# A start list written anew: two attention tiles turned by VectorE and DMA instead of TensorE, and scalings and low words on GpSimd

## The chip, the cores and the metric

The kernel runs on one core of a Trainium2 chip. Five engines work side by side, each through its own list of instructions in order: TensorE (PE; its weight loads are shown apart as PEld), VectorE (DVE), ScalarE (ACT), GpSimd (POOL) and SyncE (SP), which here only issues DMAs. ScalarE and GpSimd issue some DMAs too. The metric is the device time of one execution in microseconds (us). Before the change the median of 3 runs is 477.7 us (477.04 to 478.3).

## The reference

Attention within chunks of 64 positions, then a feed-forward layer on all 4608 tokens:

```
q, k, v: (8, 8, 576, 64)  ->  9 chunks of 64 positions per batch and head
scores = q_c @ k_c^T / 8 ;  attn = exp(scores - max) / (sum + 1e-9) ;  out = attn @ v_c
x = out as (4608, 512)
h = x @ w_in (512 x 1024) ;  e = exp(h - max) ;  sm = e / (sum e + 1e-9)
solu = h * sm ;  ln = (solu - mean) / sqrt(var + 1e-6) * g_ln
result = ln @ w_out (1024 x 512)
```

The weights arrive as 8-byte floats, 4 MB each. q, k and v are float32.

## The kernel before

The 4608 tokens are 36 tiles of 128 (two chunks of 64 each). Each tile goes through: turning q and k so that the head dimension lies on partitions; scores (64 small TensorE products); softmax; turning the probabilities; products with V; a split of x into a high and a low part; the input product (`ffn_in`, 24 TensorE products of 512 columns: high times low weights, high times high, low times high); the SoLU and its normalisation; turning z; a split of z; and the output product (`ffn_out`, 24 products, in three thirds).

There are two ways to turn. TensorE multiplies by a unit matrix into PSUM, and ScalarE or VectorE copies the outcome out. Or VectorE transposes blocks of 32 x 32 and DMAs put the blocks in place. Probabilities of the tiles below `PE_TURNED` go the first way (`attn_transpose`, word T: four TensorE transposes and four ScalarE copies per tile), the others the second (`attn_turn`, word U: one VectorE transpose per tile, and after an odd tile eight DMAs for the pair, four issued by SyncE and four by GpSimd).

From tile 5 on a loop issues the work, the same for every pair of tiles. Everything before it is issued in the order of a list, `START`: each word is a step with its tile or unit number, and a word that stands several times continues the same step. Every engine keeps the order of the list for its own instructions, its DMA issues among them. The words that matter here:

- `P:x` load weight unit x (units 0 to 3 are w_in, 4 to 7 w_out; 1 MB each); `c:x` clamp and scale it (VectorE or GpSimd, then ScalarE), `b:x` its low bits, `C:x` join, `t:x` its high word (ScalarE), `d:x` its low word;
- `n:i` load q and k of tile i as they lie in memory (`nat`, two halves used in turn), `N:i:0` and `N:i:1` turn q and k by TensorE and evict; `v:i` load V (four buffers);
- `S:i` scores, `A:i` softmax up to exp, `B:i` sum, reciprocal and scaling by it, `V:i` product with V, then the high and the low part of x;
- `M:i` input product (unit by unit for tile 0), `X:i`, `Y:i`, `R:i` SoLU, centring and variance, `z:i:h` turn half h of z by TensorE (tiles 0 and 1), `Z:i` turn z by VectorE and DMA (after tile 3: 16 DMAs), `F` the next third of an output product, `o:i` scale and store;
- `Q:2`, `q:8` the loads of q and k of batch 2 by head (`q_st`, `k_st`: 32 DMAs of 72 KB), which the tiles from 9 on read; `K:9` turns tile 9 from them;
- `w:n` n products of the unit matrix that nobody reads; `g`, `G` load and turn g_ln.

`MOVED` names the engine of some steps, where a default would be another: for evictions (N, z, V) ScalarE, for `Y` centring ScalarE, for c, b and d VectorE. `F` stands six times, so the loop starts when tiles 0 and 1 are through their output product. `ffn_in` of every tile but 1 uses one PSUM buffer (`ph`), which the multiplication in `Y` of the tile before sets free. The store of `o:i` is issued on ScalarE's own queue, in order with its other work, in the start; in the loop SyncE issues it.

In the profile almost every instruction stands under line 54, the helper through which they are recorded, so the tiles' names tell the steps apart: `nat`, `q_st`, `k_st`, `w_raw` (P), `w_a`, `w_b` (c, b, C), `wi_l`, `wo_l` (d), `sx`, `e`, `s_e` (S, A, B), `tp` (TensorE transposes and, in the loop, odd tiles' scores), `a_b` and `attn_t` (probabilities turned), `ph` (input product), `z`, `z_b`, `z_t`, `z_h`, `z_l` (z and its parts), `po` (output product).

Of the kernel before, what the change touches and what calls it, by code (L numbers as in the profile page):

```python
# [15 lines left out]


START = """
n:0 w:3 N:0:0 N:0:0 w:1 N:0:1 N:0:1 g w:1 S:0 A:0 G P:0 P:0 n:1 A:0 c:0 c:0 w:3 N:1:0 N:1:0 w:1
N:1:1 b:0 N:1:1 G P:1 w:1 S:1 B:0 v:0 C:0 A:1 t:0 T:0 T:0 c:1 c:1 w:4 V:0 V:0 P:2 b:1 c:2 n:2  # L20
d:0 P:3 A:1 n:3 w:6 N:2:0 w:1 N:2:1 C:1 V:0 B:1 t:1 c:2 T:1 N:2:0 b:2 N:2:1 T:1 d:1 S:2 n:4
M:0 M:0 C:2 t:2 c:3 c:3 v:1 A:2 A:2 b:3 d:2 C:3 N:3:0 N:3:1 N:3:1 M:0 N:3:0 S:3 N:4:0 B:2 N:4:1
t:3 N:4:0 A:3 P:5 d:3 c:5 N:4:1 A:3 T:2 T:2 S:4 V:1 M:0 P:4 n:5 B:3 T:3 V:1 V:1 M:1 X:0 X:0 T:3
A:4 A:4 b:4 v:2 N:5:1 c:4 n:6 P:7 c:5 N:5:0 c:4 Y:0 Y:0 n:7 N:5:1 V:2 b:5 v:3 B:4 N:5:0 V:2 b:7
C:4 z:0:1 P:6 v:5 N:6:0 X:1 v:4 C:5 N:6:0 S:5 Q:2 q:8 t:4 V:2 d:4 N:6:1 N:6:1 X:1 t:5 A:5 Y:1
M:2 z:0:1 z:0:1 X:2 A:5 R:0 z:0:0 z:0:0 q:8 N:7:1 q:8 c:6 S:6 Y:1 V:3 X:2 T:4 T:4 z:0:0 d:5 F
V:3 Y:2 Y:2 N:7:0 A:6 c:6 c:7 V:3 b:6 B:5 C:6 n:8 N:7:0 M:3 R:1 c:7 q:8 N:7:1 C:7 T:5 z:1:0 t:6
T:5 S:7 t:7 d:6 X:3 X:3 d:7 V:4 V:4 Y:3 Y:3 R:2 z:1:1 A:6 F F A:7 V:4 z:1:0 z:1:0 v:6 Z:2 A:7
M:4 F B:7 Z:3 o:0 V:5 z:1:1 z:1:1 B:6 F F v:7 X:4 N:8:0 X:4 U:6 U:7 V:5 Y:4 V:5 K:9 Y:4 N:8:0
R:4 R:3 N:8:1 N:8:1 o:1  # L30
"""


MOVED = """
N:0:0=dve N:8:0=dve N:8:1=dve Y:0=pool Y:1=pool Y:3=pool b:7=pool c:0=pool c:1=pool c:2=pool
c:3=pool c:4=pool c:5=pool c:6=pool c:7=pool
"""


# [23 lines left out]
def chunk_attention_then_solu_ffn(  # L63
# [18 lines left out]
    G = S // 32  # L82
# [5 lines left out]


    MS = nc.gpsimd  # L90
    PE_TURNED = 6
    PH2 = (1,)
    ORD = 5

# [12 lines left out]
    def po():  # L107
# [120 lines left out]
    def unit_low(x):  # L228
        kind, m = UNITS[x]
        a, top = scaled.pop(x), tops.pop(x)  # L230
        if kind == "in":
            dve.tensor_tensor(
                out=paired(wi_l[:, m, :]),
                in0=a.rearrange("p h (a b x) -> p (h a) x b", b=P, x=2),
                in1=top.bitcast(F32), op=ALU.subtract,
            )
            return
        for y in range(2):
            dve.scalar_tensor_tensor(
                out=wo_l[:, 2 * m + y, :], in0=a[:, y],  # L240
                scalar=g_sb[:, 2 * m + y:2 * m + y + 1], in1=top[:, y].bitcast(F32),
                op0=ALU.mult, op1=ALU.subtract,
            )
# [473 lines left out]
    def warm(n):  # L717
# [32 lines left out]
    for i in range(first, NT):  # L750
# [99 lines left out]
```

## Time and profile before

| | |
|---|---|
| median of 3 runs | 477.7 us |
| the profiled execution's own time | 477.95 us |
| its span from first to last instruction | 476.2 us |
| TensorE busy | 465.6 us (98%) |
| VectorE busy | 374.3 us (79%) |
| ScalarE busy | 256.5 us (54%) |
| GpSimd busy | 147.7 us (31%) |
| granted TensorE clock | 1.0 |
| DMA | 72.57 MB, 152 GB/s on average |

Of a group of instructions the page gives the engine, the operation, output and input by tile name, shapes and count, then the busy time and the mean of one in ns, then the engine's idle time ahead of them and what ended it. A row of the timeline has start, length, engine (SPq, POOL and ACTq for DMA issues), the same names and a count, and in brackets the idle time before it and who ended it. The row "DMA to landing" gives the time from an issue to the arrival of its data.

### The profile page before, as it was taken

What the parts mean: (1) busy time and instruction counts of PE and PEld (TensorE: products, weight loads), DVE (VectorE), ACT (ScalarE), POOL (GpSimd) and SP (SyncE); (2) the same over time, 40 slices, a digit from 0 to 9 for tenths busy, and PEclk for the clock granted to TensorE, in tenths of its full rate; (3) what the DMA queues carried; (4) which work ended last, traced back from release to release, by engine and by line L of the source; (5) the groups of instructions that cost most, each with busy time, mean ns of one, the idle gap of its engine ahead of it and who ended that gap; (6) DMA issues with size and microseconds to landing.
All of it is one profiled execution on the core that took longest, in us unless ns stands there. A gap on an engine that the chain in (4) does not pass through costs nothing.

```text
span 476.2 us, 11114 instructions
## 1 busy us (share of the span) xinstructions
PE 465.6 (98%) x4212; PEld 382.6 (80%) x4212; DVE 374.3 (79%) x520; ACT 256.5 (54%) x423; POOL 147.7 (31%) x298
## 2 busy tenths in 40 slices
PE   7899998999999999999999999999999999999997
PEld 5677786888888888888888888888888888888876
DVE  3999997798869887878787878797979797954441
ACT  2879982646444645454545455454555554545552
POOL 2212725150505050505050505032414141423330
PEclk9999999999999999999999999999999999999999
DMA  8999979758886878696358596949743435343221
GB/s 221 308 288 220 202 134 199 166 154 154 200 144 162 158 175 166 164 168 154 88 138 159 136 185 144 182 110 188 156 115 97 126 90 135 85 116 104 74 60 73
DMA packets 192924, 72.57 MB, mean 152 GB/s; under 512 B 177188, under 2 KB 177960, under 8 KB 191976
## 3 DMA queue, kind: packets, MB, share of 16 engines
q1 hardware_dynamic: 185768, 58.23, 55.4%
q0 software_dynamic: 6528, 12.86, 10.4%
q8 instruction: 33, 0.54, 0.5%
q10 hardware_dynamic: 576, 0.79, 0.5%
q14 instruction: 19, 0.16, 0.1%
HBM read 36.70 MB, written 9.44 MB: 97 GB/s over the span
## 4 chain that ended last, share of the span: by engine, by line
PE 85%; DMA 6%; SPq 3%; DVE 3%; ACT 1%; issue 1%; ACTq 0%
PE po L54 38%; PE ph L54 38%; PE tp L54 5%; PE sx L54 4%; SPq L54 3%; DMA nat<-in_k_dram 2%; DMA nat<-in_q_dram 2%; DMA z_t<-z_b 1%; DMA k_st<-in_k_dram 1%; DVE h_nmax L54 0%; DVE w_a L54 0%; DVE wo_l L54 0%; ACT attn_t L54 0%; ACT z L54 0%; ACT z_h L54 0%
## 5 line engine op out<-in xcount | busy, mean ns | idle before, releaser
L54 PE MATMUL ph<-wi_l,x_h 128*128 128x512 f32 x288 | 112.9, 392 | 1.9 <-DVE z L54 1.8
L54 PE MATMUL po<-wo_l,z_h 128*128 128x512 f32 (+1 forms) x288 | 113.3, 393 | 0.1
L54 ACT ACTIVATE z<-ph,h_nmax 128x1024 f32<-128x1024 f32 x36 | 40.2, 1117 | 134.6 <-DVE h_nmax L54 134.6
L54 PE MATMUL ph<-wi_h,x_h 128*128 128x512 f32 x288 | 112.1, 389 | 0.0
L54 PE MATMUL po<-wo_h,z_l 128*128 128x512 f32 (+1 forms) x288 | 111.9, 389 | 0.0
L54 PE MATMUL po<-wo_h,z_h 128*128 128x512 f32 (+1 forms) x288 | 111.4, 387 | 0.0
L54 POOL DMA_DIRECT2D z_t<-z_b x144 | 71.7, 505 | 28.7 <-DVE z_b L54 24.5
L54 PE MATMUL ph<-wi_h,x_l 128*128 128x512 f32 x288 | 78.1, 390 | 0.0
L54 POOL TENSOR_TENSOR u<-ssq,eps 128x1 f32<-128x1 f32 x36 | 7.1, 198 | 212.1 <-ACT sq L54 211.9
L54 DVE TENSOR_REDUCE h_nmax<-ph 128x1 f32<-128x1024 f32 x36 | 44.0, 1221 | 30.2 <-PE ph L54 30.2
L54 PEld LDWEIGHTS ph<-wi_l,x_h 128*128 128x128 f32 x288 | 54.1, 188 | 13.8 <-ACT x_h L54 2.2
L54 PEld LDWEIGHTS po<-wo_h,z_l 128*128 128x128 f32 x288 | 54.1, 188 | 12.1 <-DVE z_l L54 1.0
L54 PEld LDWEIGHTS po<-wo_l,z_h 128*128 128x128 f32 x288 | 54.1, 188 | 11.9 <-ACT z_h L54 0.5
L54 PEld LDWEIGHTS ph<-wi_h,x_l 128*128 128x128 f32 x288 | 53.9, 188 | 11.6 <-DVE x_l L54 0.4
L54 PEld LDWEIGHTS ph<-wi_h,x_h 128*128 128x128 f32 x288 | 54.1, 188 | 11.0
L54 PEld LDWEIGHTS po<-wo_h,z_h 128*128 128x128 f32 x288 | 54.1, 188 | 10.5
L54 DVE TENSOR_TENSOR z_l<-z_t,z_h 128x1024 fp32r<-128x1024 f32 (+1 forms) x37 | 42.0, 1136 | 25.3 <-ACT z_h L54 23.9
L54 DVE SCALAR_TENSOR_TENSOR z<-ph,z 128x1024 f32<-128x1024 f32 x36 | 43.9, 1219 | 13.3 <-ACT z L54 13.2
L54 ACT ACTIVATE z<-z,z_sum 128x1024 f32<-128x1024 f32 x33 | 38.1, 1154 | 23.0 <-DVE z L54 22.4
L54 DVE STREAM_TRANSPOSE z_b<-z 128x1024 f32<-128x1024 f32 x34 | 41.2, 1211 | 3.8 <-ACT z L54 3.1
L54 ACT CAST z_h<-z_t 128x1024 fp32r<-128x1024 f32 (+1 forms) x37 | 35.9, 970 | 8.6 <-PE po L54 6.5
L54 ACT ACTIVATE o_sb<-po,r 128x512 f32<-128x512 f32 (+1 forms) x36 | 24.2, 673 | 24.9 <-POOL r L54 18.6
(76 smaller groups left out, 598.6 us busy)
## 6 DMA issues: line engine op xcount, KB each, us to landing
out_dram<-o_sb SPq DMA_DIRECT2D x33, 256.0 KB, 2.5
v_sb<-in_v_dram SPq DMA_DIRECT2D x32, 256.0 KB, 4.4
z_t<-z_b POOLq DMA_DIRECT2D x128, 64.0 KB, 2.8
z_t<-z_b SPq DMA_DIRECT2D x128, 64.0 KB, 2.9
q_st<-in_q_dram SPq DMA_DIRECT2D x96, 72.0 KB, 3.1
k_st<-in_k_dram SPq DMA_DIRECT2D x96, 72.0 KB, 3.1
w_raw<-in_moe_w_out_dram SPq DMA_DIRECT2D x4, 1024.0 KB, 7.4
attn_t<-a_b POOLq DMA_DIRECT2D x60, 64.0 KB, 3.8
```

The source lines that it names most:

```text
L54: ins = make(*args, **kwargs)
```

## The change

Four things. `PE_TURNED` goes from 6 to 4, so the probabilities of tiles 4 and 5 are turned by `attn_turn`; U:4 and U:5 enter the list for T:4 and T:5. The scaling in `softmax_b` and the low word of a w_in unit in `unit_low` can be put on GpSimd by `MOVED`, which does that for B:0 to B:6, d:1 and d:3. Other entries of `MOVED` change: the clamps of units 1 and 3 go from GpSimd to VectorE, the bits of unit 4 go to GpSimd and those of unit 7 to VectorE, the centring of tile 1 to ScalarE and of tiles 3 and 4 to VectorE, some evictions change sides (N:0:1, N:1:1, N:3:0, z:1:0 and z:1:1 to VectorE, N:0:0 and N:8:1 to ScalarE). And the whole list is in another order: weight unit 1 is loaded first, unit 0 after unit 2; the loads of tile 8 (n:8) stand behind the loads of batch 2 by head; v:7 stands ahead of them; 21 unit products (w) instead of 22.

```
+START = P:1 n:0 c:1 c:1 n:1 w:6 N:0:0 b:1 w:1 N:0:1 N:0:0 P:2 C:1 t:1 w:1 N:1:0 N:1:0 N:0:1 S:0 N:1:1
+N:1:1 n:2 A:0 A:0 P:0 P:0 d:1 w:5 S:1 N:2:0 c:2 c:2 N:2:0 b:2 w:1 N:2:1 N:2:1 B:0 A:1 w:1 T:0
+C:2 b:0 c:0 A:1 T:0 S:2 c:0 g G A:2 A:2 B:1 G v:0 C:0 n:3 w:4 V:0 V:0 t:2 B:2 t:0 P:3 N:3:0
+N:3:0 n:4 w:1 N:3:1 N:3:1 v:1 T:1 T:1 V:0 T:2 S:3 d:0 b:3 M:0 T:2 c:3 A:3 N:4:0 n:5 c:3 C:3
+N:4:0 N:4:1 N:4:1 M:0 A:3 V:1 S:4 v:2 d:2 M:0 t:3 V:1 N:5:0 N:5:1 P:5 d:3 M:0 A:4 A:4 N:5:0
+N:5:1 B:3 P:4 V:1 S:5 B:4 c:5 X:0 c:4 V:2 P:6 X:0 T:3 A:5 A:5 b:5 Y:0 Y:0 c:5 M:1 z:0:0 z:0:1
+U:4 V:2 V:2 C:5 v:3 T:3 M:2 n:6 b:4 N:6:1 R:0 n:7 N:6:0 c:4 B:5 z:0:1 V:3 X:1 P:7 z:0:1 z:0:0
+z:0:0 C:4 t:5 X:1 N:7:0 t:4 v:4 Y:1 c:6 N:7:1 Y:1 v:7 N:6:1 N:6:0 d:4 N:7:0 v:5 c:7 U:5 S:6
+z:1:1 X:2 X:2 d:5 c:6 F V:3 Y:2 R:1 b:6 N:7:1 b:7 V:3 Q:2 q:8 q:8 M:3 Y:2 v:6 C:6 A:6 c:7 t:6
+q:8 q:8 C:7 d:6 t:7 S:7 X:3 V:4 d:7 z:1:0 V:4 X:3 V:4 A:6 n:8 Y:3 Y:3 F F z:1:0 z:1:0 Z:2 B:6
+A:7 o:0 z:1:1 z:1:1 R:3 Z:3 A:7 M:4 X:4 X:4 V:5 B:7 Y:4 U:6 F F U:7 Y:4 V:5 V:5 F R:2 o:1 N:8:0
+K:9 N:8:0 N:8:1 N:8:1 R:4

 MOVED = """
-N:0:0=dve N:8:0=dve N:8:1=dve Y:0=pool Y:1=pool Y:3=pool b:7=pool c:0=pool c:1=pool c:2=pool
-c:3=pool c:4=pool c:5=pool c:6=pool c:7=pool
+B:0=pool B:1=pool B:2=pool B:3=pool B:4=pool B:5=pool B:6=pool N:0:1=dve N:1:1=dve N:3:0=dve
+N:8:0=dve Y:0=pool Y:3=dve Y:4=dve b:4=pool c:0=pool c:2=pool c:4=pool c:5=pool c:6=pool
+c:7=pool d:1=pool d:3=pool z:1:0=dve z:1:1=dve

-    PE_TURNED = 6
+    PE_TURNED = 4

 (unit_low)
-            dve.tensor_tensor(
+            (pool if f"d:{x}" in moved else dve).tensor_tensor(
                 out=paired(wi_l[:, m, :]),

 (softmax_b)
-        dve.tensor_tensor(
+        (pool if f"B:{i}" in moved else dve).tensor_tensor(
             out=a, in0=e, in1=rinv.unsqueeze(2).to_broadcast([P, H, CH]), op=ALU.mult,
         )
```

The list before:

```
n:0 w:3 N:0:0 N:0:0 w:1 N:0:1 N:0:1 g w:1 S:0 A:0 G P:0 P:0 n:1 A:0 c:0 c:0 w:3 N:1:0 N:1:0 w:1
N:1:1 b:0 N:1:1 G P:1 w:1 S:1 B:0 v:0 C:0 A:1 t:0 T:0 T:0 c:1 c:1 w:4 V:0 V:0 P:2 b:1 c:2 n:2
d:0 P:3 A:1 n:3 w:6 N:2:0 w:1 N:2:1 C:1 V:0 B:1 t:1 c:2 T:1 N:2:0 b:2 N:2:1 T:1 d:1 S:2 n:4
M:0 M:0 C:2 t:2 c:3 c:3 v:1 A:2 A:2 b:3 d:2 C:3 N:3:0 N:3:1 N:3:1 M:0 N:3:0 S:3 N:4:0 B:2 N:4:1
t:3 N:4:0 A:3 P:5 d:3 c:5 N:4:1 A:3 T:2 T:2 S:4 V:1 M:0 P:4 n:5 B:3 T:3 V:1 V:1 M:1 X:0 X:0 T:3
A:4 A:4 b:4 v:2 N:5:1 c:4 n:6 P:7 c:5 N:5:0 c:4 Y:0 Y:0 n:7 N:5:1 V:2 b:5 v:3 B:4 N:5:0 V:2 b:7
C:4 z:0:1 P:6 v:5 N:6:0 X:1 v:4 C:5 N:6:0 S:5 Q:2 q:8 t:4 V:2 d:4 N:6:1 N:6:1 X:1 t:5 A:5 Y:1
M:2 z:0:1 z:0:1 X:2 A:5 R:0 z:0:0 z:0:0 q:8 N:7:1 q:8 c:6 S:6 Y:1 V:3 X:2 T:4 T:4 z:0:0 d:5 F
V:3 Y:2 Y:2 N:7:0 A:6 c:6 c:7 V:3 b:6 B:5 C:6 n:8 N:7:0 M:3 R:1 c:7 q:8 N:7:1 C:7 T:5 z:1:0 t:6
T:5 S:7 t:7 d:6 X:3 X:3 d:7 V:4 V:4 Y:3 Y:3 R:2 z:1:1 A:6 F F A:7 V:4 z:1:0 z:1:0 v:6 Z:2 A:7
M:4 F B:7 Z:3 o:0 V:5 z:1:1 z:1:1 B:6 F F v:7 X:4 N:8:0 X:4 U:6 U:7 V:5 Y:4 V:5 K:9 Y:4 N:8:0
R:4 R:3 N:8:1 N:8:1 o:1
```

More of the change, by code (lines that the diff above doesn't have):

```diff
@@ L18 @@
 START = """
[L19 to L30, printed above, removed]
+P:1 n:0 c:1 c:1 n:1 w:6 N:0:0 b:1 w:1 N:0:1 N:0:0 P:2 C:1 t:1 w:1 N:1:0 N:1:0 N:0:1 S:0 N:1:1
```

## The prediction

> **What bounds the kernel now.** I read the busy table first, then the chain of waits in order of time, then the start alone on each engine.
>
> ```profile
> PE 465.6 (98%) x4212; PEld 382.6 (80%) x4212; DVE 374.3 (79%) x520; ACT 256.5 (54%) x423; POOL 147.7 (31%) x298
> ```
>
> ```profile
> 82.15 5.68 PE ph L54 x24
> 87.83 0.72 PE sx L54 x34
> ...
> 90.27 5.70 PE po L54 x24
> ...
> 444.72 5.45 PE ph L54 x24
> ```
>
> From 82.15 us, the first product of tile 5 (first step of the loop, which the change leaves alone), the chain is TensorE piece upon piece. So the end moves with two instants: when tile 5's first product may start, and whether the products of tiles 6 and 7 with V (88.28) and the next output product (90.27) follow without a hole. Everything edited lies ahead of that.
>
> SyncE's queue is the other thing that arrives at 88 us. Its issues in the timeline (start, length):
>
> ```profile
> 50.29 0.80 SPq L54 DMA_DIRECT2D v_sb<-in_v_dram  x1
> 51.20 12.81 SPq L54 DMA_DIRECT2D q_st<-in_q_dram  x16
> 64.11 4.22 SPq L54 DMA_DIRECT2D k_st<-in_k_dram  x8
> 68.44 0.45 SPq L54 DMA_DIRECT2D nat<-in_q_dram  x1
> 69.41 0.67 SPq L54 DMA_DIRECT2D nat<-in_k_dram  x1
> 70.13 6.02 SPq L54 DMA_DIRECT2D k_st<-in_k_dram  x8
> 76.95 6.82 SPq L54 DMA_DIRECT2D z_t<-z_b  x8
> 83.87 0.53 SPq L54 DMA_DIRECT2D v_sb<-in_v_dram  x1
> 84.58 2.47 SPq L54 DMA_DIRECT2D attn_t<-a_b  x4
> ```
>
> ```profile
> DMA to landing us min/median/max: 2.0/2.5/2.9
> ```
>
> The second fence is for those four attn_t issues: the last starts near 86.5 and lands near 88.5, just when TensorE's products of tiles 6 and 7 want it. So SyncE's queue, not only TensorE, is on time to within a few tenths. Ahead of 55 us the transfers themselves are full, behind it the issue sets the pace (columns: stretch, length, busy PE, PEld, DVE, ACT, POOL, clock, DMA share, GB/s):
>
> ```profile
> 40.00:41.00 1.00, 0.45 (x4) 0.48 (x5) 0.93 (x4) 0.81 (x1) 1.00 (x1) 1.00 0.20 43
> 50.00:55.00 5.00, 5.00 (x90) 4.14 (x88) 4.38 (x8) 4.19 (x11) 2.57 (x4) 1.00 1.07 289
> 60.00:65.00 5.00, 4.82 (x87) 4.04 (x87) 5.00 (x7) 4.71 (x10) 0.64 (x1) 1.00 0.73 117
> ```
>
> **The change part by part.** *Tiles 4 and 5.* Two groups of four TensorE transposes go, and eight ScalarE copies (two groups of 1.5 us):
>
> ```profile
> 52.06 0.66 PE L54 MATMUL tp<-ident,s_e 128*128 128x128 f32 x4
> 52.48 0.48 PE L54 MATMUL po<-wo_l,z_h 128*128 128x512 f32 x1
> 52.76 1.51 ACT L54 COPY attn_t<-tp 64x256 f32<-64x256 f32 x4
> 79.41 1.29 DVE L54 STREAM_TRANSPOSE a_b<-e 128x512 f32<-128x512 f32 x2
> ```
>
> From start to next start a group costs TensorE 0.42 us, so both 0.84 us. In their place come two VectorE block transposes (the last row, 1.29 us) and eight DMAs, four on SyncE (2.47 us by the row above), four on GpSimd.
>
> *Work moved from VectorE to GpSimd and back.* Rows:
>
> ```profile
> L54 DVE TENSOR_TENSOR s_e<-e,s_rinv 128x512 f32<-128x512 f32 x6 | 4.2, 692 | 0.2
> L54 DVE TENSOR_TENSOR wi_l<-w_a,wi_h 128x1024 fp32r<-128x1024 f32 x4 | 4.9, 1216 | 0.0
> L54 POOL TENSOR_SCALAR w_a<-w_raw 128x1024 f32<-128x1024 f32 x8 | 10.3, 1289 | 31.0 <-DMA w_raw<-in_moe_w_in_dram 18.4 <-DMA w_raw<-in_moe_w_out_dram 10.3 <-DVE z L54 2.3
> L54 POOL TENSOR_SCALAR w_b<-w_raw 128x1024 uint32<-128x1024 uint32 x1 | 3.7, 3729 | 6.6 <-DVE s_nmax L54 6.6
> L54 DVE TENSOR_SCALAR w_b<-w_raw 128x1024 uint32<-128x1024 uint32 x7 | 5.9, 841 | 0.3 <-DMA w_raw<-in_moe_w_in_dram 0.3
> ```
>
> VectorE gives up seven scalings and two low words: at most 7 x 0.69 + 2 x 1.22 = 7.3 us. It takes two clamps (at its own w_b row 0.84 each), two z evictions and one more N eviction (0.69), two centrings (0.84 to 1.22) and U:4, U:5 (1.3): 7 us. So VectorE's total is unchanged; what changes is the order. GpSimd has no two-input row of this size; by its one-input rows a scaling of 512 lies between 0.64 (half of 1289) and 1.86 (half of 3729), a low word of 1024 between 1.3 and 3.7. I take 1.2 and 2.3, nearer the clamp because both are float: 13 us on an engine that is busy under a third. The scaling stands between exp and the transpose, so each costs its attention chain 0.5 us more than on VectorE; it is hidden as long as TensorE has other list work, and it has.
>
> [...]
>
> ```profile
> 36.82 1.48 DVE L54 TENSOR_SCALAR w_b<-w_raw 128x1024 uint32<-128x1024 uint32 x1
> 39.36 0.68 DVE L54 TENSOR_SCALAR w_b<-w_raw 128x1024 uint32<-128x1024 uint32 x1
> ```
>
> ```profile
> 36.65 1.10 POOL L54 TENSOR_SCALAR w_a<-w_raw 128x1024 f32<-128x1024 f32 x1 [1.47 <-DMA w_raw<-in_moe_w_out_dram]
> ```
>
> *The new order on TensorE.* Unit 0 is now loaded after units 1 and 2 and tiles 0 to 2, as the last of 4.5 MB. The page's slices of 11.9 us moved
>
> ```profile
> GB/s 221 308 288 220 202 134 199 166 154 154 200 144 162 158 175 166 164 168 154 88 138 159 136 185 144 182 110 188 156 115 97 126 90 135 85 116 104 74 60 73
> ```
>
> so 221 x 11.9 = 2.6 MB in the first, and the other 1.9 MB take 6.2 us at 308: its bytes are in at some 18.1 us, near 18.5 with the landing. VectorE's list then holds b:0, A:2 (two operations), the sums and reciprocals of B:1 and B:2, C:0, an eviction, V:0 and d:0: by 0.69 for what is 512 wide, 1.22 for 1024, 0.2 for a reciprocal, 0.7 + 1.4 + 1.8 + 1.2 + 0.7 + 0.7 + 1.2 = 7.7 us. So the first product starts near 26 us, against 23.36:
>
> ```profile
> 23.36 0.50 PE L54 MATMUL ph<-wi_l,x_h 128*128 128x512 f32 x1
> 34.21 0.48 PE L54 MATMUL ph<-wi_l,x_h 128*128 128x512 f32 x1
> 40.55 1.06 PE L54 MATMUL tp<-ident,nat 128*128 128x128 f32 x8 [0.62 <-DMA nat<-in_k_dram]
> 41.55 0.69 PE L54 MATMUL sx<-attn_t,v_sb 64*64 64x64 f32 x32
> 42.17 0.66 PE L54 MATMUL tp<-ident,z 128*128 128x128 f32 x4
> 82.15 0.47 PE L54 MATMUL ph<-wi_l,x_h 128*128 128x512 f32 x1 [1.84 <-DVE z L54]
> ```
>
> Tile 1's product (34.21 before) comes near 37, 2.8 us later; but by then N:5, V:2 and S:5 are done, which stood behind it (1.00 and 0.62 us from start to start, S:5 taken as V:2), T:4 and T:5 are gone (0.84), and the waits of 1.84 and 0.62 us need not recur. TensorE itself could thus start tile 5's product at 82.15 + 2.8 - 2.2 - 0.8 - 2.5 = 79.4; if the first product is as early as before but for a us, 77.6.
>
> *The new order on SyncE.* This decides. Into the list ahead of the 32 head loads (q_st, k_st) come v:7 and U:5's four issues; n:8 goes from between them to behind all of them. Up to 55 us bytes count: v:7 is 0.25 MB and U:5 0.5 MB, at the 289 GB/s above 0.9 + 1.7 us. A dry moment like 40:41 (share 0.20) loses 0.8 us; before, SyncE had to wait for a tile half still unread, and the new list asks for the halves later against their reading. I count 1.9 us given back; none and four such moments (3.3 us) are the ends. So the head loads start 0.7 us later, -0.7 to +2.6. They keep 0.53 us each (4.22 over 8). With n:8 not between them they end 1.8 us earlier (68.3 to 70.13), which n:8 spends again before the z_t issues; these shift by +0.7, and the split of tile 2 that wants them begins only at 88.31 now, 4 us behind the last of them. The attn_t issues lose v:7 ahead of them (84.58 - 83.77 = 0.8) and with less backlog some of the 1.5 us by which 70.13's eight exceeded 64.11's eight (6.02 against 4.22, I count 0.6): +0.7 - 0.8 - 0.6 = -0.7 us. n:8 lands 3.8 to 4.4 us after issue:
>
> ```profile
> DMA to landing us min/median/max: 3.8/4.1/4.4
> ```
>
> It is issued near 75.5 to 76.5, so it lands near 80; N:8 stands before tile 5's product in TensorE's list, so that product starts at 80 to 81, whatever TensorE has gained. Its 5.7 us end at 86.5, and the V products wait until the attn_t landing, 88.5 - 0.7 = 87.8.
>
> **Sum.** What TensorE gains, some 3 us, becomes a wait for SyncE's queue, and the end shifts by -0.7 us: span 476.2 - 0.7 = 475.5. The profiled execution took 477.95, 1.75 us around its span, and its own time is 0.25 above the median 477.7; I predict 475.5 + 1.75 - 0.25 = 477.0. With the ends above the shift is -0.7 - 1.4 = -2.1 to -0.7 + 1.9 = +1.2; 475.6 to 478.9.
>
> **Rivals.** *The queue keeps ahead.* If the head loads run at 0.53 us without the stalls of before (52 + 32 x 0.53 + 0.7 for v:6 + 1.2 for n:8 = 70.9, and 4.1 to land), n:8 is in at 75, and TensorE's own 77.6 to 79.4 holds: 82.15 - 78.4 = 3.8 us saved, 477.7 - 3.8 = 473.9. For it: the list now asks for tile halves only long after they are free, so the dry moments vanish. Against it: U:5 stands in that queue.
>
> *U:5 arrives late* (the other sign). SyncE reaches U:5's DMAs near 51 to 52 and everything named above is queued behind them: 32 head loads, n:8, z_t and attn_t. U:5 on VectorE needs tile 5 scaled by GpSimd, behind b:4 there (3.73 us by the row), and d:4 on VectorE; by VectorE's list I get 49 to 51. Every us beyond 52 is a us at the end. With contention as at 36.82 on a handful of instructions and 1.8 us for a scaling, U:5 comes at 54 to 55: +2.7 us, 477.7 + 2.7 = 480.4. Against it: the moves leave VectorE's total alone.
>
> *The store on ScalarE.* In the new list the second output store (o:1) stands ahead of N:8:1's eviction and R:4 on ScalarE. Before, that store held ScalarE until 87.39 and the split of tile 2 to 88.31:
>
> ```profile
> 87.39 0.34 ACTq L630 DMA_DIRECT2D out_dram<-o_sb  x1
> 88.31 1.05 ACT L54 CAST z_h<-z_t 128x1024 fp32r<-128x1024 f32 x1 [2.08 <-DMA attn_t<-a_b]
> ```
>
> If it is held as long again, an eviction (0.59) and R:4 (1.4) now follow it, and the output product waits: +1.8 us, 479.5. For it is only that the store waits for an earlier transfer on record; if that is a z_t one, it is through by 85.
>
> **How the numbers follow.** Forecast 0.45, queue ahead 0.27, U:5 late 0.20, store 0.08. About 0.3% (1.43 us) is what a measurement of this kernel can tell from no change: 476.3 and 479.1 are the bounds. Of the forecast's 0.45 I put 0.12 below, 0.29 inside, 0.04 above; of the queue-ahead case nine tenths below; of U:5 late four fifths above; of the store half. Faster 0.12 + 0.25 = 0.37, slower 0.04 + 0.16 + 0.04 = 0.24, the rest 0.39. The forecast's own range is 475.6 to 478.9; the whole one reaches past the faster case (TensorE at 77.6 gives 473.1) and the slower one: 472.9 to 480.8.
>
> **What would show it.** Right: TensorE reaches N:8 by 78 or 79, stands idle there or before the V products until about 88, released by a DMA (nat or attn_t), and the output product begins near 89.5. The first ph product at about 26 us and tile 1's near 37 check the order; GpSimd's scalings at 0.64 to 1.86 us check the costs. U:5's first SyncE issue behind an idle longer than a us would mean the slower rival; tile 5's product before 80 without a DMA wait behind it the faster one. The prediction is wrong if the steady loop behind 90 us gets holes that it doesn't have now, since all of the above is ahead of it.

## The result and the profile after

The changed kernel takes 482.05 us (median of 11 runs, 478.85 to 484.3), the kernel before beside it 476.49 us (11 runs, 474.99 to 479.19). The ratio of the two, estimated over all runs, is 1.0101 with a 95% interval of 1.0076 to 1.0126 (the medians alone give 1.2%). It is slower by 1.0%, above the whole forecast range. Measured again with other kernels it was 479.91 against 475.74 us, ratio 1.0109 (1.0085 to 1.0133).

The profiled execution took 484.2 us with a span of 482.4, 6.2 more than before. First the page of the changed kernel (busy times, and the granted clock in 40 slices), then its chain of waits:

```profile
PE 467.0 (97%) x4202; PEld 383.4 (79%) x4202; DVE 374.1 (78%) x520; ACT 252.0 (52%) x412; POOL 158.6 (33%) x307
...
PEclk9999999799999999999999999999999999999999
```

```profile
79.70 6.25 DMA nat<-in_k_dram
87.12 7.12 PE ph L55 x24
96.45 5.66 PE po L55 x24
```

Busy times hardly move; VectorE's total is what the prediction said. The chain has something new: a DMA (nat, the load n:8) stands in it, tile 5's input product behind it lasts from 86.77 to 94.24, 7.5 instead of 5.7 us (the 7.12 of the chain's row counts from 87.12 only), and the output product starts at 96.45 instead of 90.27. That is 6.2 us, the whole of the difference; behind it every piece lasts as long as before. The "7" in the clock row is the same place. TensorE alone there, from its timeline, and the stretches around (columns as in the prediction: busy PE, PEld, DVE, ACT, POOL, granted clock, DMA share, GB/s):

```profile
84.23 1.09 PE L55 MATMUL tp<-ident,nat 128*128 128x128 f32 x4 [2.87 <-DMA nat<-in_q_dram]
86.00 1.12 PE L55 MATMUL tp<-ident,nat 128*128 128x128 f32 x4 [0.68 <-DMA nat<-in_k_dram]
```

```profile
80.24:83.65 3.41, 1.12 (x5) 0.58 (x4) 2.64 (x4) 3.41 (x10) 3.11 (x7) 1.00 1.04 241
...
83.60:83.80 0.20, 0.00 (x0) 0.00 (x0) 0.20 (x3) 0.20 (x3) 0.20 (x2) 0.62 1.20 254
90.40:90.60 0.20, 0.20 (x2) 0.20 (x1) 0.20 (x1) 0.20 (x1) 0.00 (x0) 0.81 0.90 174
```

TensorE stands idle for 2.87 us at N:8. During that idle, at 83.65 us, the clock falls from 1.00 to 0.50, and it comes back at 90.47: the shares 0.62 and 0.81 of the two 0.2-us stretches place the edges, 6.83 us apart. Tile 5's product starts 4.6 us later than before (86.77 against 82.15), and at half clock it lasts about 1.8 us longer.

Why nat is late is seen on SyncE's queue (start and length of the issues):

```profile
48.39 7.06 SPq L55 DMA_DIRECT2D v_sb<-in_v_dram  x4
55.55 3.66 SPq L55 DMA_DIRECT2D q_st<-in_q_dram  x5
59.39 2.67 SPq L55 DMA_DIRECT2D attn_t<-a_b  x4
62.10 6.49 SPq L55 DMA_DIRECT2D q_st<-in_q_dram  x11
68.63 0.50 SPq L55 DMA_DIRECT2D v_sb<-in_v_dram  x1
69.17 9.93 SPq L55 DMA_DIRECT2D k_st<-in_k_dram  x16
79.15 0.51 SPq L55 DMA_DIRECT2D nat<-in_q_dram  x1
79.70 1.43 SPq L55 DMA_DIRECT2D nat<-in_k_dram  x1
81.23 5.88 SPq L55 DMA_DIRECT2D z_t<-z_b  x8
87.22 2.44 SPq L55 DMA_DIRECT2D attn_t<-a_b  x4
```

The head loads begin at 55.55 instead of 51.20, four V loads ahead of them having taken 7.06 us; U:5's four issues stand in their midst with 2.67 us; the first k_st goes out at 69.17 instead of 64.11 and n:8 at 79.15. (The list has U:5 ahead of all head loads. SyncE did not keep that order: five q_st issues stand ahead of U:5's in the repetition's profile too, and no run shows why.) The attn_t issues of tiles 6 and 7 follow at 87.22 instead of 84.58.

### The profile page after: what moved, and what is told of

Read it like the earlier page. It is cut to its first block, busy times and chain, and to the rows that moved or that the text cites. A ratio compares the mean times of both kernels' runs of the same rounds, so it can differ in the third digit from the quotient of the medians.

```text
span 482.4 us, 11110 instructions
## 1 busy us (share of the span) xinstructions
PE 467.0 (97%) x4202; PEld 383.4 (79%) x4202; DVE 374.1 (78%) x520; ACT 252.0 (52%) x412; POOL 158.6 (33%) x307
## 4 chain that ended last, share of the span: by engine, by line
PE 81%; DMA 6%; SPq 4%; DVE 2%; ACT 2%; POOL 2%; issue 1%; ACTq 0%; POOLq 0%
PE po L55 38%; PE ph L55 36%; SPq L55 4%; PE tp L55 4%; PE sx L55 4%; DMA nat<-in_q_dram 3%; DMA w_raw<-in_moe_w_out_dram 2%; DMA nat<-in_k_dram 1%; POOL w_b L55 1%; ACT z L55 1%; DVE h_nmax L55 0%; ACT w_a L55 0%; DVE wo_l L55 0%; DVE z L55 0%; DVE w_a L55 0%
## 5 line engine op out<-in xcount | busy, mean ns | idle before, releaser
L55 POOL TENSOR_TENSOR u<-ssq,eps 128x1 f32<-128x1 f32 x36 | 8.3, 231 | 219.8 <-ACT sq L55 219.6
```

The source lines that it names most:

```text
L55: ins = make(*args, **kwargs)
```

## The experiments

Theory A: SyncE's queue sets both the start of tile 5's product and the products with V. Theory B: an engine is late by itself (ScalarE held by its own store, or GpSimd's new work). Theory C: the idle halves the clock, and that is part of the loss. The table has all results; "start" is when tile 5's input product begins, "output" when the output product behind the V products does, and "span" the time from first to last instruction, all three of the profiled execution. The sets were measured on several chips, so compare the ratios and not the medians.

| kernel | median us | ratio to before | 95% interval | start | output | span |
|---|---|---|---|---|---|---|
| before (first profile) | | | | 82.15 | 90.27 | 476.2 |
| changed (first profile) | 482.05 | 1.0101 | 1.0076–1.0126 | 86.77 | 96.45 | 482.4 |
| after_again | 479.91 | 1.0109 | 1.0085–1.0133 | 81.89 | 91.70 | 477.7 |
| warm_n8 | 480.15 | 1.0084 | 1.0054–1.0114 | 84.72 | 92.63 | 478.5 |
| n8_early | 480.91 | 1.0105 | 1.0069–1.0141 | 85.46 | 95.75 | 481.8 |
| store_pool | 482.6 | 1.0130 | 1.0094–1.0167 | 85.16 | 94.78 | 480.9 |
| n8_store | 482.24 | 1.0143 | 1.0123–1.0164 | 79.59 | 93.52 | 480.5 |
| n8_v7_store | 482.06 | 1.0135 | 1.0109–1.0161 | 79.38 | 92.33 | 479.3 |
| queue_only | 478.93 | 1.0062 | 1.0050–1.0074 | 81.89 | 90.80 | 476.5 |
| queue_free | 479.07 | 1.0077 | 1.0059–1.0094 | 81.48 | 89.45 | 476.5 |
| queue_c7 | 477.84 | 1.0053 | 1.0033–1.0073 | 80.84 | 89.39 | 475.7 |
| turn45 | 481.79 | 1.0124 | 1.0091–1.0157 | 86.43 | 94.31 | 480.0 |
| no_pool | 481.3 | 1.0118 | 1.0102–1.0133 | 86.18 | 94.07 | 481.2 |
| order_only | 486.61 | 1.0225 | 1.0212–1.0238 | 91.40 | 99.32 | 485.0 |
| before_pool | 478.4 | 1.0070 | 1.0056–1.0085 | 82.75 | 90.63 | 476.3 |
| before_turn | 493.22 | 1.0362 | 1.0336–1.0388 | 97.54 | 105.43 | 491.4 |
| before_turn_g | 487.31 | 1.0247 | 1.0219–1.0276 | 92.58 | 100.47 | 486.3 |
| before_store | 475.42 | 0.9992 | 0.9973–1.0011 | 80.45 | 88.37 | 474.2 |

In 14 rows span less output is 385.7 to 386.3: the loop behind is as rigid as the prediction took it. The other four are near 387; in n8_store and n8_v7_store the half clock reaches into the output product, and in queue_free and no_pool the loop has a hole of 0.5 to 0.6 us, a wait of TensorE for z_l near 140 us. The median of the kernel before is 475.3 to 475.8 us in the sets from which all rows but the first two come, so its first profile (477.95 us) shows an execution above its median.

**The clock: warm_n8.** Six products of the unit matrix fill TensorE's wait.

```
-A:7 o:0 ... F F U:7 Y:4 V:5 V:5 F R:2 o:1 N:8:0
+A:7 o:0 ... F F U:7 Y:4 V:5 V:5 F R:2 o:1 W:6 N:8:0
+    def warm_bank(n):
+        m = ident.unsqueeze(1).to_broadcast([P, 4, P])
+        pt = bank().rearrange("p (x m) -> p x m", m=P)
+        for _ in range(n):
+            pe.matmul(pt, ident, m, start=True, stop=True)
```

> The changed kernel with six products of the unit matrix (128x512 each, 3 us in all, result not used) on TensorE just ahead of N:8's transposes, in the idle time in which it waits for nat. Theory C (the idle of 2.9 us halves the granted clock for the next 7 us, and 1.9 of the 6.2 us come from that): the granted clock stays near 1.0 in 83 to 92 us, tile 5's 24 products take 5.6 instead of 7.5 us, the V products then wait for attn_t until 92.4 (94.24 before), and the time falls by 1.5 to 1.9 us with less spread between runs. If the clock falls for another reason than the idle, nothing changes (within 0.5 us).

Its timeline on TensorE, and one stretch of it:

```profile
78.78 5.31 PE L55 MATMUL tp<-ident 128*128 128x512 f32 x12
83.93 1.04 PE L55 MATMUL tp<-ident,nat 128*128 128x128 f32 x8
84.72 0.48 PE L55 MATMUL ph<-wi_l,x_h 128*128 128x512 f32 x1
```

```profile
88.00:89.00 1.00, 1.00 (x6) 0.83 (x5) 0.32 (x1) 0.89 (x3) 0.46 (x2) 1.00 0.77 255
```

(Each of the six stands as two records.) The clock stays at 1.00 through tile 5's product, and its chain's output product comes at 92.63. All six runs show a mean clock of 0.998 to 1.0 and lie within 479.45 to 481.29; of 17 runs of the changed kernel 9 lie above 481.3, and all nine have a clock of 0.993 or 0.996. In the repetition (after_again) the two at 482.4 and 482.95 have 0.993, the other four (0.996 to 0.999) lie at 479.5 to 480.3. So every run above 481.3 had lost clock, though not every run that lost clock lies there. In the repetition the two cost 2 to 3 us more, which holds the longer wait as well as the clock behind it. The medians of the two kernels differ by 0.2%, inside the intervals: the gain of theory C in the median is not shown, and what these six runs show is that the upper end is gone. At 0.88 us a product the filling lasted 5.3 us and not the 3 that I had counted. It ended at 84.1, while n:8's second load went out at 77.1; at the 4.4 us of the slowest such load in the profile before (4.7 in the repetition's, from 76.75 to 81.4) it was in at 81.5 to 81.8. So by my estimate the filling itself held N:8 up by some 2 us, as much as the clock could give back.

> The changed kernel as it is, for the comparison on one chip with the runs beside it: 1.0 to 1.4% slower than the kernel before; tile 5's product near 86 behind a wait for nat, the granted clock at 0.5 for some 7 us behind that wait.

Its profile is one of the early runs (479.47 us): nat landed at 81.4, waits of 1.31 and 0.55 us, no loss of clock, tile 5's product at 81.89 and not near 86; then the V products wait for attn_t and the output product comes at 91.70:

```profile
90.08 0.63 PE L55 MATMUL sx<-attn_t,v_sb 64*64 64x64 f32 x27 [1.54 <-DMA attn_t<-a_b]
```

**Three waits one behind the other: n8_early, store_pool, n8_store, n8_v7_store.** n:8 back among the head loads; the early stores issued by GpSimd; both; both and v:7 behind the head loads.

```
n8_early:
-q:8 q:8 C:7 d:6 t:7 S:7 X:3 V:4 d:7 z:1:0 V:4 X:3 V:4 A:6 n:8 Y:3 Y:3 F F z:1:0 z:1:0 Z:2 B:6
+q:8 n:8 q:8 C:7 d:6 t:7 S:7 X:3 V:4 d:7 z:1:0 V:4 X:3 V:4 A:6 Y:3 Y:3 F F z:1:0 z:1:0 Z:2 B:6
store_pool (store_rest):
-            (sync if order.on and len(stores) == 1 else nc.scalar).dma_start(to, of)
+            (nc.gpsimd if not order.on else sync if len(stores) == 1 else nc.scalar).dma_start(to, of)
n8_store: both;  n8_v7_store: both, and v:7 moved from behind "c:6 N:7:1 Y:1" to ahead of "Y:3 Y:3 F F"
```

> The changed kernel with one word moved: n:8 (the two nat loads of tile 8) stands between the third and the fourth group of head loads again, as in the kernel before. Theory A (SyncE's queue sets both instants): the nat loads are issued near 73.5 us instead of 79.2 and land by 78.5, so TensorE reaches N:8 at about 81.4 without a wait and tile 5's first product starts at 82.4 at full clock, ending at 88; but the z_t and attn_t issues stand where they stood, so the products with V wait for attn_t until about 92.4 and the output product starts near 94.5 instead of 96.45. Time: 1.5 to 2 us below the changed kernel (480), or no change at all if that second wait halves the clock in its turn. Theory B (only the place of n:8 was wrong): no wait takes its place, the output product starts at 90.5, 6 us less (476).

> The changed kernel with the two output stores of the start issued by GpSimd instead of ScalarE, so that ScalarE is not held from 70 to 78.6 us and from 84.3 to 88.7. Theory A (SyncE's queue): R:3, A:7's exp and X:4's exp come 3 to 8 us earlier, but nat still lands at 84 to 86 and attn_t at 92, so tile 5's product still starts at 85.5 to 87 and the time stays within 1 us. Theory B (ScalarE held by its own store is what is late): tile 5's product starts 3 us or more earlier and the time falls by 3 to 6 us.

> The changed kernel with both n:8 back between the third and the fourth group of head loads and the two output stores of the start issued by GpSimd. Theory: three things stood one behind the other at 82 to 86 us, the landing of nat, the exp and centring of tile 4 (late because ScalarE was held by its own store; with n:8 alone moved they released tile 5's product only at 85.5) and TensorE's own list (80.4 to 81.4). With the first two gone tile 5's product starts at 80.5 to 82 at full clock; then the next wall comes, the landing of the last attn_t at 88 to 90, so the output product starts at 90.5 to 92 instead of 96.45 and the time is 477 to 479. Rival: the store only shifts its wait to GpSimd, which stands ahead of tile 5's z and attn_t DMAs, and tile 5's product still starts behind 84: 480 to 482.

> The changed kernel with n8 back among the head loads, the two early stores by GpSimd and v:7 behind the head loads; U:5 as in the change (four on SyncE among the head loads). Theory: v:7's stall (4 us in the changed kernel's profile) goes, the last k_st lands at 82 to 84 and the last attn_t at 87 to 89 instead of 85.5 and 90.7, so tile 5's product stays near 80 and the output product starts at 87 to 90: 3 to 5 us below the changed kernel, 475 to 478, about the kernel before. If U:5's issues are what counts and not v:7: 480 to 482 as with n8 and the stores alone.

TensorE in n8_early, in store_pool (two rows) and in n8_store (four rows):

```profile
85.46 0.77 PE L55 MATMUL ph<-wi_l,x_h 128*128 128x512 f32 x1 [4.06 <-DVE z L55]
```

```profile
82.07 1.09 PE L55 MATMUL tp<-ident,nat 128*128 128x128 f32 x4 [2.45 <-DMA nat<-in_q_dram]
84.39 1.12 PE L55 MATMUL tp<-ident,nat 128*128 128x128 f32 x4 [1.23 <-DMA nat<-in_k_dram]
```

```profile
79.59 0.48 PE L55 MATMUL ph<-wi_l,x_h 128*128 128x512 f32 x1
...
86.94 0.69 PE L55 MATMUL sx<-kT,qT 64*64 64x64 f32 x32 [1.65 <-DVE qT L55]
89.41 0.44 PE L55 MATMUL sx<-attn_t,v_sb 64*64 64x64 f32 x2 [1.77 <-DMA attn_t<-a_b]
90.68 1.02 PE L55 MATMUL sx<-attn_t,v_sb 64*64 64x64 f32 x27 [0.83 <-DMA attn_t<-a_b]
```

With n:8 early the wait for nat is gone and one of 4.06 us takes its place, for tile 4's z: ScalarE's exp and with it VectorE's multiplication come late because ScalarE is held by its store. In the changed kernel that hold reads

```profile
79.05 0.29 ACT L55 ACTIVATE eps<-h_sum,tiny 128x1 f32<-128x1 f32 x1 [8.69 <-DMA k_st<-in_k_dram]
```

that is, the store itself waits for a head load. Freeing ScalarE alone (store_pool) leaves the wait for nat: theory B falls as the sole cause, as theory A said. ("The store waits for a head load" is the profile's own attribution of the wait; no run tests it.) With both gone tile 5's product starts at 79.59, where the prediction's sum for TensorE alone had it (79.4) and 2.6 us before that of the first profile of before, and still the time does not move: the last k_st (for K:9's turn, in VectorE's order ahead of N:8's eviction, which the scores wait for) and attn_t are late, and the clock is halved from 88.8 to 95.6 (0.50 in the stretches from 90 to 95). Theory A stood by its mechanism; its numbers for n8_store (output at 90.5 to 92, 477 to 479 us) were too good by 1.5 us at the output and 3 us in time, since the waits behind the product (1.65, 1.77 and 0.83 us in the rows above) cost clock as the one of 2.87 us ahead of it did in the changed kernel. n8_v7_store was a miss: without v:7 in the way the last k_st lands earlier, but the attn_t issues still start at 85.99 and the time stays. The place of v:7 alone is not what decides.

**SyncE's queue relieved: queue_only, queue_free, queue_c7.** U:5's four SyncE issues go to GpSimd and v:7 behind n:8; then also n:8 early and the stores by GpSimd; then also U:5 ahead of c:7, whose clamp held its DMAs up on GpSimd.

```
queue_only (attn_turn; v:7 as in n8_v7_store):
-                        (pool if x == y else sync).dma_start(
+                        (pool if x == y or i == 5 else sync).dma_start(
queue_free: queue_only + n8_store;   queue_c7: queue_free with
-z:0:0 C:4 t:5 X:1 N:7:0 t:4 v:4 Y:1 c:6 N:7:1 Y:1 N:6:1 N:6:0 d:4 N:7:0 v:5 c:7 U:5 S:6
+z:0:0 C:4 t:5 X:1 N:7:0 t:4 v:4 Y:1 c:6 N:7:1 Y:1 N:6:1 N:6:0 d:4 N:7:0 v:5 U:5 c:7 S:6
```

> The changed kernel with less in SyncE's queue ahead of the nat loads of tile 8 and nothing else touched: the four attn_t issues of U:5 go to GpSimd too (eight there), and v:7 stands behind n:8 instead of ahead of the head loads. Theory A (SyncE's queue decides): the head loads and n:8 are issued 3 to 5 us earlier, nat lands at 79 to 82, the wait of 2.9 us shrinks to under 1 us, so no clock is lost; then tile 4's exp and centring, held up by ScalarE's store, are next, with tile 5's product at 82.5 to 85: 2 to 4 us below the changed kernel. If SyncE's queue is not what decides, within 1 us of it.

> As the run with less in SyncE's queue, and also n:8 back among the head loads and the two early stores issued by GpSimd. With these two alone tile 5's product started at 79.6 us, but the last k_st landed at 85.5 and attn_t at 90.7, and the output product started at 93.5 at half clock. Theory A: without U:5 and v:7 in SyncE's queue these land 3 to 5 us earlier, so the products with V follow tile 5's product with under 1 us of wait, the clock stays full and the output product starts at 86.5 to 88.5: 5 to 7 us below the changed kernel, 475 or a little less. Rival (the waits there come from VectorE or GpSimd, which has eight DMAs more to issue): the output product stays behind 91, 479 to 482.

> The run with the freed queue (U:5's eight DMAs on GpSimd, v:7 behind the head loads, n:8 among them, the early stores by GpSimd), and U:5 one word ahead of c:7, so that GpSimd issues U:5's DMAs at 52.7 instead of 55.7 us and unit 7's clamp behind them. Theory A: the wait of 1.73 us in front of tile 5's V products goes, tile 5's first loop product starts at 79.6 to 80, and if z_t and attn_t move with it the output product starts at 87.5 to 88.5: 475 to 477, level with the kernel before (475.7) or up to 1 us under it. Rival: attn_t of tiles 6 and 7 stays at 86 to 87 or the loads of the loop behind it take the lead back (with the freed queue alone a lead of 0.8 us at 90 was gone by 163): 477.5 to 479 as with the freed queue alone.

SyncE in queue_only:

```profile
48.13 13.64 SPq L55 DMA_DIRECT2D q_st<-in_q_dram  x16
61.87 2.01 SPq L55 DMA_DIRECT2D v_sb<-in_v_dram  x1
63.97 9.37 SPq L55 DMA_DIRECT2D k_st<-in_k_dram  x16
73.44 0.44 SPq L55 DMA_DIRECT2D nat<-in_q_dram  x1
```

n:8 goes out at 73.44 instead of 79.15 (76.21 in the repetition's profile); the time falls from 1.0109 to 1.0062 of the kernel before on the same chip, with intervals that do not meet, and all five runs lie within 478.24 to 479.0. So what stands in SyncE's queue is part of the cause, with the clock that goes with the waits. Its size is less sure: by the ratios 0.47 of 1.09%, 2.2 us, the lower end of the 2 to 4 expected; by the medians 1 us, which is where theory A and its rival meet. Which of the two words counts is not settled. In time it looks like U:5's DMAs: with n:8 early and the stores by GpSimd, taking v:7 away brought nothing (1.0143 and 1.0135), taking U:5 away as well brought 1.0077 (queue_free). But in the traces the 16 q_st take as long without U:5's issues among them (13.64 us) as with them (14.1 us in the repetition, from 51.65 to 65.77); what comes earlier is their start, 48.13 instead of 51.65. queue_free adds nothing more in time. With eight DMAs on GpSimd tile 5's V products wait in both (1.93 us in queue_only; 1.73 us in queue_free, released by attn_t at 64.17); queue_free's output product still comes 1.35 us earlier, but that lead is lost again in the loop behind (span less output is 387.05 against 385.7; 0.53 us of it is the hole). queue_c7 takes the wait at 64 us away, but VectorE's late x_l puts one of 1.34 us at 59.01 in its place, and it ends at 1.0053. Its output product starts at 89.39 at full clock. No version of the new order reached the kernel before, and what the last 0.5% hang on is left open.

**The parts one by one.** turn45 undoes the first part in the new order, no_pool the second, order_only both. before_turn and before_turn_g put the first part alone into the old order (as in the change, and with U:5's DMAs and the early stores all by GpSimd), before_pool the second.

```
turn45:
-N:5:1 B:3 P:4 V:1 S:5 B:4 c:5 X:0 c:4 V:2 P:6 X:0 T:3 A:5 A:5 b:5 Y:0 Y:0 c:5 M:1 z:0:0 z:0:1
-U:4 V:2 V:2 ...
+N:5:1 B:3 P:4 V:1 S:5 B:4 c:5 X:0 c:4 V:2 P:6 X:0 T:3 A:5 A:5 b:5 Y:0 Y:0 c:5 M:1 T:4 T:4 z:0:0 z:0:1
+V:2 V:2 ...          (and "c:7 U:5 S:6" -> "c:7 T:5 T:5 S:6", PE_TURNED = 6)
no_pool:     MOVED without B:0 to B:6, d:1 and d:3
order_only:  turn45 and no_pool together
before_turn: old list, "T:4 T:4" -> "U:4", "T:5 z:1:0 t:6 T:5" -> "U:5 z:1:0 t:6", PE_TURNED = 4
before_turn_g: before_turn with queue_only's line and store_pool's line
before_pool: old list, MOVED with B:0 to B:6, d:1 and d:3 on pool
```

> The changed kernel with its first part undone: tiles 4 and 5 are turned by TensorE and ScalarE again (T:4 T:4 and T:5 T:5 near the places of U:4 and U:5), so SyncE issues no attn_t<-a_b among the head loads. Theory A (SyncE's queue): everything behind is issued some 2.7 us earlier, nat lands at 83 and attn_t at 89.7; TensorE has 0.84 us more to do; tile 5's product starts at 83 to 84 after a wait of under 1.5 us, so the clock stays full, and the output product starts at 91.7 to 92: 4 to 5 us below the changed kernel (477.5). Theory B (the engines' own work is late, above all ScalarE): eight copies more on ScalarE make it no better, 0 to +1 us.

> The changed kernel with its second part undone: the seven scalings and the two low words of units 1 and 3 are VectorE's again, in the new order. Theory A (VectorE has no slack ahead of 60 us, and what it finishes late keeps buffers and SyncE's loads waiting): 7 us more on VectorE push tile 5's turn, and with it everything on SyncE, back: 2 to 4 us slower than the changed kernel (484 to 486). Theory B (the moves are what made the changed kernel slow, through GpSimd's longer scalings and VectorE's instructions that last 1.6 to 1.9 instead of 0.7 to 1.2 us beside GpSimd): it is faster by 1 to 4 us (478 to 481).

> The changed kernel with both parts undone, so that only the new order (and the new places of the evictions, clamps and centrings) is left: tiles 4 and 5 turned by TensorE and ScalarE, scalings and low words by VectorE. Each part undone alone left the time 1.2% above the kernel before. If the new order by itself is what is slow (first product 2.6 us later, tile 1's 4.3 us later, with T:4 and T:5 added to TensorE again): 1 to 1.5% above the kernel before. If the two parts only hide each other's cost: within 0.5% of it.

> The kernel before with the second part alone: its own order, T:4 and T:5 by TensorE, and the seven scalings and the low words of units 1 and 3 by GpSimd. Theory A (what GpSimd does longer is hidden behind TensorE's list work, and the new order's SyncE queue is what cost the time): within 1 us of the kernel before. Theory B (the moves cost by themselves): 2 to 6 us slower, with waits of TensorE for attn_t released by ScalarE or GpSimd in 30 to 65 us.

> The kernel before with the first part alone: U:4 and U:5 in the old places of T:4 and T:5, four of U:5's DMAs on SyncE (the planner puts them behind all 32 head loads, ahead of v:6 and the z_t issues), four on GpSimd. Theory A (SyncE's queue): the last attn_t of tile 5 lands near 80, the products V:4 and V:5 and all behind them wait for it, z_t and the attn_t of tiles 6 and 7 come 2.5 us later too: 3 to 7 us slower than the kernel before, with a TensorE wait released by attn_t in 72 to 80 us. Theory B (the first part is a gain by itself, 0.84 us of TensorE and 3 us of ScalarE): 0.5 to 1 us faster.

> As the run before it, with all eight DMAs of U:5 and the two early output stores issued by GpSimd, so that SyncE's queue is that of the kernel before. Theory A: the attn_t of tile 5 lands at 75 to 77 and the wait in front of V:4 is 0 to 3 us; z_t and the next attn_t are as before: between 1 us faster and 2 us slower than the kernel before. If the place in SyncE's queue was not what cost, it is as slow as the run before it.

TensorE in turn45, then in before_turn and before_turn_g:

```profile
45.50 0.63 PE L55 MATMUL tp<-ident,z 128*128 128x128 f32 x4 [1.64 <-ACT attn_t L55]
47.51 1.11 PE L55 MATMUL tp<-ident,z 128*128 128x128 f32 x4 [1.37 <-ACT attn_t L55]
...
60.31 0.66 PE L55 MATMUL tp<-ident,z 128*128 128x128 f32 x4 [1.06 <-ACT attn_t L55]
```

```profile
77.15 0.44 PE L54 MATMUL sx<-attn_t,v_sb 64*64 64x64 f32 x2 [15.98 <-DMA attn_t<-a_b]
```

```profile
69.28 0.45 PE L54 MATMUL sx<-attn_t,v_sb 64*64 64x64 f32 x2 [4.51 <-DMA attn_t<-a_b]
73.54 1.13 PE L54 MATMUL sx<-attn_t,v_sb 64*64 64x64 f32 x30 [3.81 <-DMA attn_t<-a_b]
```

In turn45 theory B came out, by its number (no better; by the ratios about 1 us worse) and by its engine. SyncE was early there (n:8 at 72.41), as A said, but TensorE itself came late: it waits 4.07 us in these three places for ScalarE's copies of attn_t, so tile 5's product starts at 86.43 without any DMA wait. The first part thus takes about 5 us off TensorE's path in the new order (4.07 and the 0.84 of the prediction), not 0.84; as the time is no better for it, as much is lost elsewhere, in the changed kernel's profile at nat and at the clock.

The new order by itself is the slowest of its kind, 1.0225. Each part alone brings it to 1.012, both to 1.010 or 1.011, so the parts are gains of 5 us there that do not add up. The profiles show a reason: with only one of them TensorE reaches tile 5's product at 86.2 to 86.4 us, behind waits for nat of 1.57 us in no_pool and behind none in turn45, and with both it is there early and waits for nat (1.86 to 3.55 us). order_only missed its 1 to 1.5%, and no_pool (level with the changed kernel) both of its theories. In the old order the same parts are losses. The GpSimd moves cost 0.7%, 3.3 us, as theory B of that run had it; its profile has TensorE waiting for POOL's s_e and wi_l in four places from 21 to 35 us, 1.6 us in all, of which the longest is the row below; what makes up the rest of the 3.3 us is not shown.

```profile
24.50 0.50 PE L55 MATMUL ph<-wi_l,x_h 128*128 128x512 f32 x1 [0.51 <-POOL wi_l L55]
```

The turn costs 3.6%, far more than the 3 to 7 us expected. There U:5's issues stand behind 32 head loads on SyncE, the V products ahead of everything else on TensorE: 15.98 us of idle. With all eight DMAs and the stores on GpSimd, SyncE as before, 8.3 us of waits remain; so the place in SyncE's queue is about half of the waits, and by the time a third of the loss (1.2 of 3.6%). The rest I put down to the longer way through VectorE and DMA, which no run tests by itself; "0 to 3 us" for it was a miss.

**Looking for a version that beats both: before_store.** The kernel before with the early stores issued by GpSimd (store_pool's line).

> The kernel before with the two output stores of the start issued by GpSimd. Theory (ScalarE is held by its store from 69.5 to 75.0 us and that is what the 1.84 us of idle before tile 5's product hang on): this idle goes, tile 5's product starts near 80.5; the V products then wait for the landing of attn_t at 88.5, so the output product comes at 89.8 to 90.3 instead of 90.27: 0 to 0.5 us faster; more, up to 1.8 us, if attn_t too comes earlier because GpSimd and ScalarE are free sooner. Rival (the idle hangs on VectorE's own list): the same time within 0.3 us and the idle stays.

The 1.84 us of idle ahead of tile 5's product go, as the theory had it; output product at 88.37. The time is the same as before (ratio 0.9992, 0.9973 to 1.0011): a gain of up to 0.5 us could not be told apart here, one of 1.8 us is not there. That wait may be one of the profiled execution alone: in this set the kernel before has spans of 472.8 to 474.7 us in 14 of 15 executions, and the 386 us of the loop behind put their output product at 87 to 88.7 too, not at the 90.27 of the first profile. None of these was profiled. No version beat both kernels.

## Why the prediction was wrong

**What held.** The bound: behind the output product nothing changed. The reading that SyncE's queue decides and that TensorE would stand at N:8, released by nat: it did, exactly there. TensorE's own gain held too: it reached N:8 at 81.4 us in the first profile and at 79.0 in the repetition's, against "78 or 79". The first product "near 26" and GpSimd's scaling (1.2 taken) and low word (2.3 taken) held, tile 1's product "near 37" is 1.5 us late, all in the changed kernel:

```profile
25.96 0.50 PE L55 MATMUL ph<-wi_l,x_h 128*128 128x512 f32 x1
...
38.52 0.48 PE L55 MATMUL ph<-wi_l,x_h 128*128 128x512 f32 x1
```

```profile
L55 POOL TENSOR_TENSOR s_e<-e,s_rinv 128x512 f32<-128x512 f32 x4 | 5.0, 1262 | 4.0 <-DVE s_rinv L55 2.5 <-DVE g_sb L55 1.4
L55 POOL TENSOR_TENSOR wi_l<-w_a,wi_h 128x1024 fp32r<-128x1024 f32 x2 | 4.8, 2418 | 17.2 <-ACT wi_h L55 17.2
```

**The step that failed** is the SyncE term, "So the head loads start 0.7 us later, -0.7 to +2.6. They keep 0.53 us each", and behind it the attn_t term. The prediction counted v:7 as 0.9 us and U:5 as 1.7 us of bytes, both ahead of the head loads, and gave 1.9 us back for the dry moments. In the first profile the head loads begin 4.35 us later, without U:5. The four V loads ahead of them take 7.06 us, one issue alone 4.07 (shortest, median and longest in ns):

```profile
L55 SPq DMA_DIRECT2D v_sb<-in_v_dram x4: 612/1096/4065, 48.4 to 51.4; - x4
```

From there to n:8's issue it is 23.6 us, as counted (from 51.9 to 75.5 or 76.5): the 2.67 us of U:5's issues in the midst of the head loads and the 0.62 us of each k_st (9.93 over 16) are made up by the q_st, 10.15 us for 16 instead of 12.81. So it is the start of the head loads that makes n:8's issue late, 79.15 instead of 75.5 to 76.5. What holds SyncE for these 4 us stays open: with v:7 gone from there (n8_v7_store) the V loads take 1.95 us, but the first five q_st 6.05 instead of 3.66. n:8 then lands in 4.9 to 6.25 instead of 3.8 to 4.4 us, and tile 5's product starts at 86.77 instead of 80 to 81.

In the repetition's profile the head loads begin at 51.65, n:8 goes out at 76.21 and the product starts at 81.89: the prediction's figure plus a microsecond, so the term varies by 3 us from run to run. And still that run took 479.47 us, above the forecast's own range, because the attn_t term (-0.7) failed: "the V products wait until the attn_t landing, 88.5 - 0.7 = 87.8". SyncE issued the four attn_t even earlier than that, 1.1 us ahead of the profile before:

```profile
83.44 2.60 SPq L55 DMA_DIRECT2D attn_t<-a_b  x4
```

```profile
DMA to landing us min/median/max: 4.1/4.2/4.6
```

But the tile's eight attn_t DMAs (SyncE's four and GpSimd's four) landed after 4.1 to 4.6 us instead of the 2.0 to 2.9 that the prediction took over from the profile before, so the V products went on at 90.08 and the output product began at 91.70 instead of near 89.5. The DMA share from 86 to 90 us is 1.04 to 1.32 there against 0.69 to 0.71 before; that the fuller transfers are the reason is not shown.

The sum also started from an execution above the median. The profile before was taken at 477.95 us, and the median of that kernel was 475.3 to 476.5 in every later set, so some of the waits that the prediction wanted to win (1.84 us at tile 5) may not be there in most executions.

**What the sum did not have** is the clock: a wait of TensorE was priced at its own length, and the 2.87 us at N:8 in the first profile cost about 1.8 us more behind them, at a clock of 0.50.

**Prices that were too small.** The 0.84 us for T:4 and T:5: in the new order the waits for ScalarE's copies are 4 us more of it. The scaling on GpSimd, "hidden as long as TensorE has other list work": in the new order the moves cost nothing that could be measured (no_pool), in the old one 0.7%. The argument that "VectorE's total is unchanged; what changes is the order" was true and missed the point, because the order by itself costs 2.2% and only the two parts make it bearable.

**The rivals.** "The queue keeps ahead" did not happen. "U:5 late" gave the right sign and about half the size (+2.7 us, against 4.2 and 5.6 by the medians) by the wrong mechanism: VectorE turned tile 5 at 52.5 us, but SyncE did not stand idle ahead of U:5's issues; it reached them at 59.39 behind its own head loads. "The store on ScalarE" did hold ScalarE (8.69 us at o:0 and 4.81 at o:1), and store_pool shows that this alone decides nothing; it is the wait that appears when nat's is taken away.

**A reading that does not carry.** The rival "U:5 late" counts with "contention as at 36.82", where VectorE's w_b lasted 1.48 us beside a GpSimd clamp, against the 0.68 us at 39.36. Beside the row of 0.68 us GpSimd was at work too, with a centring, in the kernel before:

```profile
39.55 1.49 POOL L54 TENSOR_SCALAR z<-z,z_sum 128x1024 f32<-128x1024 f32 x1 [1.80 <-DVE z L54]
```

So the two w_b rows do not show that work on GpSimd makes VectorE's longer, and no run shows the term by itself. In the changed kernel one w_b beside a GpSimd clamp took 1.56 us (at 13.24) and another 0.69 (at 18.16), and tile 5 was turned at 52.5 us instead of 54 to 55. The forecast did not use the term.

## What to carry to other kernels

When a queue and an engine arrive at the same instant, price an added DMA by the place at which the queue will reach it (bytes where the transfers are full, as from 50 to 55 us before with 289 GB/s at a DMA share of 1.07; issue time where they are not, as from 64 to 68 us with 0.53 us an issue at shares of 0.73 to 0.79), follow everything behind it, and do not take the time to landing over from a profile of another order (2.0 to 2.9 us became 4.1 to 4.6); a gain upstream of the queue turned here into waits of 1.86 to 3.55 us. Taking away the first wait of several that lie within 3 us of each other shows little, so free the queue itself or take all of them away together. A new order and a new division of work are not to be priced apart: here each part was worth 5 us in one order and cost 3 to 17 us in the other.

## What the runs showed of the hardware

In the changed kernel a wait of TensorE of 2.87 us was enough to halve its clock, from 1.00 to 0.50: the edge at 83.65 lies 2.3 us into the wait. In the repetition's profile waits of 1.31 and 0.55 us brought no drop. The half clock lasted 3.41 us in n8_v7_store and 6.83, twice that, in the changed kernel, so I count TensorE's work in stretches of 3.41 us. The one ahead of the edge holds 1.12 us of work in the changed kernel (the row 80.24:83.65 above); in n8_v7_store it holds 0.98, and the 3.41 us ahead of those, with 1.92, brought no drop:

```profile
83.86:87.27 3.41, 1.92 (x38) 1.27 (x36) 1.24 (x2) 0.00 (x0) 0.29 (x1) 1.00 0.63 193
87.27:90.68 3.41, 0.98 (x47) 0.91 (x51) 2.38 (x3) 1.05 (x1) 0.00 (x0) 0.99 0.53 125
...
90.60:90.80 0.20, 0.20 (x24) 0.20 (x18) 0.20 (x2) 0.00 (x0) 0.00 (x0) 0.59 1.26 285
94.00:94.20 0.20, 0.20 (x2) 0.13 (x2) 0.20 (x1) 0.20 (x1) 0.00 (x0) 0.88 0.08 13
```

(The last two rows place the edges in n8_v7_store, at 90.64 and 94.05.) Half a clock over 3.41 or 6.83 us of 480 is 0.004 or 0.007, which is where the mean clocks of 0.996 and 0.993 come from. No run shows that the hardware itself counts in such stretches; what was measured ahead of the drop in the changed kernel is 2.3 us of idle beside 1.12 us of work.
